# Another order of the first steps, and one pair in four turned by VectorE, in a fused attention and feed-forward kernel

## The chip, the cores and the metric

The kernel runs on one core of one Trainium2 chip. The metric is the device time of one execution in microseconds (us). A core has TensorE (PE in the profile, its weight loads PEld), VectorE (DVE), ScalarE (ACT), GpSimd (POOL) and SyncE (SP), which each work through their own list of instructions in order, and 16 DMA engines that they share.

## The reference

Attention inside chunks of 64 tokens, then a feed-forward block on its result:

```python
scores = scale * np.matmul(q_c, k_c.transpose(0, 1, 2, 4, 3))   # 8 x 8 heads, 576 tokens, chunks of 64, depth 64
scores = scores - np.max(scores, axis=-1, keepdims=True)
attn = np.exp(scores)
attn = attn / (np.sum(attn, axis=-1, keepdims=True) + 1e-09)
out = np.matmul(attn, v_c)
...
xn = (x - mu) / np.sqrt(var + 1e-06) * g_ln                     # x: 4608 tokens x 512
ch = np.maximum(xn @ w_ch1, 0.0) @ w_ch2                        # 512 -> 2048 -> 512
return (x + ch).astype(np.float32)
```

All inputs are float32. The weights reach the kernel as 64-bit words, of which the chip puts the low and the high half together again, and products are made from a high and a low part of each operand, three matmuls for one.

## The kernel before

The 4608 tokens are 18 pairs of 256 tokens, two pairs are a tile, nine tiles in all. The first three tiles (LEAD = 3, pairs 0 to 5) go through an ordinary feed-forward network, in three stretches of program: START, SECOND and THIRD. The other six tiles are done in three units of two tiles, four pairs, each, with a scheme that saves products by sums and differences of blocks.

**Attention** is a generator (`attention`, lines 264 to 560). Each `yield` ends a step, so a caller that holds the generator decides what stands between its steps. The steps of a pair: load q and k; 64 small matmuls for the scores (line 312, into the PSUM tile `s`); the row maxima `top` (line 319) and the load of v; the subtraction and exponential; the turning of the probabilities `p_sb` into `pt_sb`; the sums `den`; 64 small matmuls with the values (line 413); the division into `x`; the statistics (lines 457 and 458); the scaling `xg` (line 469); for the pairs of the units after the first, ScalarE's scaling by `rstd` (line 475), one transpose of 32x32 blocks on VectorE (line 480) and 16 DMAs that put the blocks into `rows`. There are three ways to turn the probabilities. For the first pairs (`by_pe`) TensorE does 8 transposes and ScalarE two copies (lines 362 and 364). In the units TensorE does it in two steps (`pt_by_pe`, lines 372 and 375), or VectorE does it in four steps of four transposes each of 32x256 (line 384). Pairs 0 and 1 (streams a and b) subtract the maxima by a matmul with `minus` (line 339) and take the sums from the matmul with the values, and their `xg` is turned by TensorE (line 522, ScalarE copies at line 525, low parts by line 529 and 532).

**Weights.** `convert_w` (stream w, lines 157 to 241) fetches the blocks in parts (part 0 and 1 are the halves of block 0 and have 512 KB each, part i is block i - 1 and has 1 MB), takes the absolute value on ScalarE (`start_w`, line 171), rounds on VectorE (`round_w`, lines 178, 179 and 182), sets the sign (`sign_w`, line 189) and casts to the high part on ScalarE (line 195); for parts 2 to 10 ScalarE writes the negative of it (line 197) and a GpSimd DMA adds the rounded value to make the low part (`split_w`, line 212); for parts 0 and 1 TensorE does the subtraction (lines 208 and 209). Three raw places and three places for the rounded values are used in turn.

**START** is a string in which each character takes one step of a stream: a and b are the attention of pairs 0 and 1, A and B of pairs 2 and 3, E of pair 4, w the weights, k two matmuls that only keep TensorE busy (`keep_warm`, line 245), u, v and y the products of the feed-forward network (u for pair 0 and v for pair 1 in blocks 0 to 5, y for both from block 6), and 1, 2 and 3 the rectifying and splitting that belongs to u, v and y. A product stream makes the first-layer block 0 and 1 (line 569), the second-layer part of block 0 (line 593), the first-layer block 2, the second-layer part of block 1, and so on. Instructions reach each engine's list in the order of the string. A tile that takes another's place waits until every reader of the other is done.

**Units.** `unit_ffn` makes 4 quarters of 14 products (line 1022), each 6 matmuls of 512 columns, and then 28 pairs of items of the second layer (`double.products`, line 952), 24 matmuls of 256 columns for each pair of items. It counts its work: 6 a product, 3.17 a quarter of a pair of items, 691 in all for one unit. `weave` takes the steps of other streams when the count has passed the position that is written down for them. In unit u the four pairs of unit u + 1 are prepared: pair n begins at BEGINS[n] and its steps stand at BEGINS[n] + PAIR_STEPS[n]; the tuple's length says which way the probabilities are turned (17 steps by TensorE, 19 by VectorE). The load of q and k of the next pair is taken at the begin of each pair. HALVES are the positions at which `combine` makes the operands of the next unit from the turned rows (512 and 612). VectorE's own part of a quarter is six adds (line 1031) and two mixes (line 1039); in the second layer it splits each item (`low`, lines 894 and 898), as a plan says (`double.plan`): item i is rounded (`high`) at i - 4 and split at i - 3.4.

Of the kernel before, what the change touches and what calls it, by code (L numbers as in the profile page):

```python
# [31 lines left out]

START = "kkwkwakwbkwkwkawwwwaawwbwabbkwAkwawbwakkabkkaabaAbabauw1Abbub1Bkbwvuuwuw12wwAvvvw22AwvwvuAvw2wwAvvw1u2AuwwBwvuv12vBuuwyywABA1ww3Ayww3wAywAyuwwwwA3y3BywBBBwBEyyBBwy3w3yywBwwyww3BwwyByy3ywy33yy3E"
LEAD = 3
UNITS = (NTILE - LEAD) // 2

# [10 lines left out]
}  # L49
ROOMS = {1: (3, 9), 2: (6,)}  # L50

BEGINS = (4, 92, 154, 246)
STEPS = (0, 5, 9, 14, 20, 31, 42, 53, 61, 67, 72, 77, 85, 90, 97, 104, 116, 128, 140)
BY_TENSOR = (0, 6, 11, 18, 33, 37, 40, 48, 54, 60, 67, 72, 80, 86, 98, 110, 122)
WIDE = (0, 5, 9, 14, 22, 35, 48, 61, 69, 75, 80, 85, 93, 98, 105, 110, 122, 134, 146)
AT_END = (0, 6, 11, 18, 33, 37, 40, 48, 54, 82, 92, 97, 104, 109, 121, 133, 146)
PAIR_STEPS = (STEPS, BY_TENSOR, WIDE, AT_END)
HALVES = ((512, 8), (612, 10))
MIXING = ((8, 10, 14, 18, 40, 48, 50, 64), (64, 66, 70, 74, 84, 92, 94, 108))
REST = (2, 6, 20)  # L60
# [43 lines left out]
def chunk_attention_ffn(ctx: ExitStack, tc: tile.TileContext, qkv, v01, g, w, out):  # L104
# [1017 lines left out]
    def play(order, streams):  # L1122
        for c in order:
            next(streams[c])
# [33 lines left out]
    with tc.manual_schedule():  # L1158
        nc.scalar.activation(minus, ident, AF.Copy, scale=-1.0)
        play(START, now)  # L1160
        now.update(
# [10 lines left out]
        def following(u, n):  # L1172
            n, u = n % 4, u + n // 4
            if (u, n) not in streams and u < UNITS:
                by_pe = len(PAIR_STEPS[n]) == len(BY_TENSOR)
                streams[u, n] = tiles[LEAD + 2 * u + n % 2].attention(n // 2, pt_by_pe=by_pe)
            return streams.get((u, n), iter(" "))
# [7 lines left out]
        for u in range(UNITS):  # L1185
            if u + 1 < UNITS:
                for n in range(4):
                    begin, steps = BEGINS[n], PAIR_STEPS[n]
                    side += [(begin + at, following(u + 1, n)) for at in steps]
# [41 lines left out]
```

## Time and profile before

| | us |
|---|---|
| median of 3 runs | 827.74 (827.0 to 831.5) |
| the profiled execution | 827.4 |
| its span | 825.6 |
| TensorE busy | 815.5 |
| VectorE busy | 624.4 |
| ScalarE busy | 346.6 |
| GpSimd busy | 202.9 |

The span runs from the first to the last instruction that the hardware profiler recorded. A row of a group gives line, engine, operation, tiles, shapes and count, then the busy time, the mean of one in ns, the idle time of the engine just before and what ended it. A row of the timeline begins with the start in us and the duration in us (several equal instructions are merged, x says how many); what stands in square brackets is the idle time before it and the releaser. The chain of waits lists start, length and what the time was spent on. In the windows each engine has its busy time in the stretch. The granted clock was 0.999 in this run.

### The profile page before, as it was taken

What the parts mean: (1) busy time and instruction counts of PE and PEld (TensorE: products, weight loads), DVE (VectorE), ACT (ScalarE), POOL (GpSimd) and SP (SyncE); (2) the same over time, 40 slices, a digit from 0 to 9 for tenths busy, and PEclk for the clock granted to TensorE, in tenths of its full rate; (3) what the DMA queues carried; (4) which work ended last, traced back from release to release, by engine and by line L of the source; (5) the groups of instructions that cost most, each with busy time, mean ns of one, the idle gap of its engine ahead of it and who ended that gap; (6) DMA issues with size and microseconds to landing.
All of it is one profiled execution on the core that took longest, in us unless ns stands there. A gap on an engine that the chain in (4) does not pass through costs nothing.

```text
span 825.6 us, 16930 instructions
## 1 busy us (share of the span) xinstructions
PE 815.5 (99%) x6746; PEld 711.8 (86%) x6746; DVE 624.4 (76%) x999; ACT 346.6 (42%) x553; POOL 202.9 (25%) x172
## 2 busy tenths in 40 slices
PE   7999999999999999999999999999999999999998
PEld 5888888888888888888899997888999988889998
DVE  6989975787566975879688988797889942249954
ACT  4766432131333432443464542434544532345432
POOL 0111005553857966510000450000002700000000
PEclk9999999999999999999999999999999999999999
DMA  9998315958786349988789669687796586668662
GB/s 359 334 290 231 153 52 192 357 191 282 266 300 224 116 153 384 345 276 281 279 256 345 188 198 345 227 279 255 225 314 210 179 295 192 197 186 291 209 212 102
DMA packets 114366, 201.66 MB, mean 244 GB/s; under 512 B 8432, under 2 KB 75504, under 8 KB 110320
## 3 DMA queue, kind: packets, MB, share of 16 engines
q1 hardware_dynamic: 112992, 195.87, 69.5%
q0 software_dynamic: 1296, 4.72, 2.9%
q8 instruction: 53, 0.87, 0.4%
q14 instruction: 25, 0.20, 0.1%
HBM read 142.88 MB, written 48.76 MB: 232 GB/s over the span
## 4 chain that ended last, share of the span: by engine, by line
PE 92%; DVE 4%; DMA 2%; issue 0%; ACT 0%; SPq 0%; DVEq 0%; ACTq 0%
PE y L952 29%; PE y L1022 26%; PE y L593 15%; PE h L569 15%; PE s L312 2%; PE h L413 1%; DMA wp<-wfs 1%; DMA qk<-qkv 1%; DVE pt_sb L384 1%; PE s L413 1%; PE s L339 0%; PE s L372 0%; PE s L362 0%; DVE hu L1031 0%; PE s L501 0%
## 5 line engine op out<-in xcount | busy, mean ns | idle before, releaser
L1022 PE MATMUL y<-xc,ring 128*128 128x512 f32 x1008 | 235.1, 392 | 0.2 <-DVE hu L1031 0.2
L1022 PEld LDWEIGHTS y<-xc,ring 128*128 128x128 f32 x1008 | 187.5, 188 | 39.8 <-DVE hu L1031 0.6
L952 PE MATMUL y<-ring,hx 128*128 128x256 f32 x1272 | 158.0, 283 | 0.0
L952 PEld LDWEIGHTS y<-ring,hx 128*128 128x128 f32 x1272 | 155.0, 192 | 0.0
L569 PE MATMUL h<-xth,wp 128*128 128x512 f32 (+1 forms) x432 | 129.5, 370 | 0.8 <-DMA wp<-wfs 0.8
L1031 DVE TENSOR_TENSOR hu<-y,snap 128x512 f32<-128x512 f32 x72 | 49.2, 686 | 68.5 <-PE y L1022 34.1
L593 PE MATMUL y<-wp,hh 128*128 128x512 f32 x376 | 96.2, 394 | 0.0
L889 ACT ACTIVATE hx<-hu 128x512 fp32r<-128x512 f32 x106 | 65.6, 630 | 68.0 <-PE y L952 59.9
L569 PEld LDWEIGHTS h<-xth,wp 128*128 128x128 f32 x432 | 78.2, 188 | 15.4 <-DMA wp<-wfs 1.0
L794 POOL TENSOR_TENSOR xc<-rows,xc 128x512 fp32r<-128x512 f32 x28 | 59.9, 2152 | 113.7 <-ACT xc L790 112.1
L593 PEld LDWEIGHTS y<-wp,hh 128*128 128x128 f32 x376 | 69.1, 188 | 13.9
L898 DVE TENSOR_TENSOR hx<-hu,hx 128x512 fp32r<-128x512 f32 x90 | 67.4, 757 | 16.7 <-ACT hx L889 15.2
L569 PE MATMUL h<-xtl,wp 128*128 128x512 f32 (+1 forms) x216 | 78.3, 367 | 0.0
L1028 ACT COPY snap<-y 128x512 f32<-128x512 f32 x72 | 41.6, 585 | 72.0 <-PE y L1022 72.0
L952 PE MATMUL y<-ring,hh 128*128 128x256 f32 x496 | 71.8, 283 | 0.0
L583 DVE SCALAR_TENSOR_TENSOR hl<-h,hh 128x512 fp32r<-128x512 f32 (+1 forms) x53 | 32.9, 627 | 50.1 <-ACT hh L582 49.9
L582 ACT ACTIVATE hh<-h 128x512 fp32r<-128x512 f32 (+1 forms) x53 | 28.6, 546 | 97.5 <-PE h L569 97.4
L952 PEld LDWEIGHTS y<-ring,hh 128*128 128x128 f32 x496 | 65.2, 192 | 0.2
L463 POOL TENSOR_TENSOR rstd<-vare,mhalf 128x2 f32<-128x2 f32 x12 | 10.0, 832 | 175.3 <-DVE vare L462 175.3
L889 ACT ACTIVATE hh<-hu 128x512 fp32r<-128x512 f32 x62 | 38.7, 631 | 31.5 <-PE y L952 28.3
L593 PE MATMUL y<-wp,hl 128*128 128x512 f32 x188 | 51.8, 390 | 0.0
L384 DVE STREAM_TRANSPOSE pt_sb<-p_sb 32x256 f32<-32x256 f32 x112 | 48.8, 436 | 3.6 <-ACT p_sb L348 1.7
(147 smaller groups left out, 1087.9 us busy)
## 6 DMA issues: line engine op xcount, KB each, us to landing
ring<-wa SPq DMA_DIRECT2D x84, 512.0 KB, 5.0
ring<-wb SPq DMA_DIRECT2D x48, 512.0 KB, 4.2
ring<-w2d SPq DMA_DIRECT2D x36, 512.0 KB, 4.0
raw<-w SPq DMA_DIRECT2D x15, 1024.0 KB, 7.8
out<-x SPq DMA_DIRECT2D x22, 512.0 KB, 5.5
qk<-qkv SPq DMA_DIRECT2D x18, 512.0 KB, 6.9
w2d<-wp SPq DMA_DIRECT2D x16, 512.0 KB, 7.5
wa<-parts SPq DMA_DIRECT2D x32, 256.0 KB, 5.5
```

The source lines that it names most:

```text
L384: nc.vector.transpose(out=pt_sb[quad(2 * h2 + j), :, c, quad(i)], in_=p_sb[quad(2 * c + i), :, h2, quad(j)])
L569: nc.tensor.matmul(h, lhsT=(wh, wh, wl)[m][:, ks], rhs=(xth, xtl, xth)[m][:, k, :], start=i == 0, stop=i == len(terms) - 1,)
L582: nc.scalar.activation(hh, h, AF.Relu)
L583: nc.vector.scalar_tensor_tensor(out=hl, in0=h, scalar=0.0, in1=hh.bitcast(F32), op0=ALU.max, op1=ALU.subtract)
L593: nc.tensor.matmul(sums(pairs[j // 2])[j % 2], lhsT=(hh, hh, hl)[m], rhs=(wh, wl, wh)[m], start=f == 0 and m == 0, stop=f == NF - 1 and m ...
L794: engine.tensor_tensor(out=o[:, 1], in0=x, in1=o[:, 0].bitcast(F32), op=ALU.subtract)
L889: nc.scalar.activation(hh, self.split[i][2], AF.Relu if x == "1" else AF.Copy)
L898: nc.vector.tensor_tensor(out=hl, in0=x, in1=hh.bitcast(F32), op=ALU.subtract)
L952: nc.tensor.matmul(bank[j // 2][:, j % 2 * PAIR : (j % 2 + 1) * PAIR], lhsT=(hh, hh, hl)[m][:, j * P : (j + 1) * P], rhs=loaded[t // 2][:, ...
L1022: nc.tensor.matmul(bank, lhsT=w[:, (0, 0, 1)[m], ks], rhs=x[:, (0, 1, 0)[m], k, :], start=start and k == m == 0, stop=k == 1 and m == 2, s ...
L1028: nc.scalar.copy(out, bank)
L1031: nc.vector.tensor_tensor(out=out, in0=bank, in1=s, op=ALU.add)
```

## The change

The first 125 or so characters of START are in another order (three k fewer; from `ww3Ayww3` on the two strings are equal). The load of pair 0 is issued ahead of the first weights, one of the k steps behind it; the turning of pair 0's probabilities comes ahead of the fourth part's absolute value; all turning steps of pair 0's `xg` come before pair 1's division; and pair 1's first transposes stand ahead of the first product of u. In the units the second pair uses STEPS instead of BY_TENSOR, so VectorE turns its probabilities in four steps, and the third and fourth pair begin at 190 and 282 instead of 154 and 246, with steps as before.

```diff
-START = "kkwkwakwbkwkwkawwwwaawwbwabbkwAkwawbwakkabkkaabaAbabauw1Abbub1Bkbwvuuwuw12wwAvvvw22AwvwvuAvw2wwAvvw1u2AuwwBwvuv12vBuuwyywABA1ww3Ayww3wAywAyuwwwwA3y3BywBBBwBEyyBBwy3w3yywBwwyww3BwwyByy3ywy33yy3E"
+START = "awkwkwkbkkwwkawwkwwkawabwawAbbawwbwwakkbaaaaaAbabbbuw1ABub1bwkbuuvwuw1v2wwAvvw22AwvvAvvwwAu2vwwuwv21AuwwwBuuy12BvvA1wuAywBww3Ayww3wAywAyuwwwwA3y3BywBBBwBEyyBBwy3w3yywBwwyww3BwwyByy3ywy33yy3E"
...
-BEGINS = (4, 92, 154, 246)
+BEGINS = (4, 92, 190, 282)
 STEPS = (0, 5, 9, 14, 20, 31, 42, 53, 61, 67, 72, 77, 85, 90, 97, 104, 116, 128, 140)
 BY_TENSOR = (0, 6, 11, 18, 33, 37, 40, 48, 54, 60, 67, 72, 80, 86, 98, 110, 122)
 WIDE = (0, 5, 9, 14, 22, 35, 48, 61, 69, 75, 80, 85, 93, 98, 105, 110, 122, 134, 146)
 AT_END = (0, 6, 11, 18, 33, 37, 40, 48, 54, 82, 92, 97, 104, 109, 121, 133, 146)
-PAIR_STEPS = (STEPS, BY_TENSOR, WIDE, AT_END)
+PAIR_STEPS = (STEPS, STEPS, WIDE, AT_END)
```

## The prediction

> **What bounds the kernel now.** I read the page first, then TensorE's list of waits from 60 us to the end, then the chain of waits, and last the instructions in order of time, for the first 60 us and for the second unit.
>
> ```profile
> span 825.6 us, 16930 instructions
> PE 815.5 (99%) x6746; PEld 711.8 (86%) x6746; DVE 624.4 (76%) x999; ACT 346.6 (42%) x553; POOL 202.9 (25%) x172
> PE y L1022 <- DVE hu L1031: 0.2, 1, 0.2
> ```
>
> The third line is the whole list of TensorE's waits after 60 us. From there on TensorE is the bound, and its work comes off the time one for one, as long as no new wait opens. Ahead of 60 us the chain of waits looks different:
>
> ```profile
> 2.11 6.86 DMA qk<-qkv
> 44.38 9.65 DMA wp<-wfs
> 66.82 1.43 PE h L569 x12
> 92.42 1.09 PE s L413 x64
> ```
>
> It runs through pair 0's load and VectorE's list, and that part ends in the transfer that adds block 4's low half in (split_w, line 212). The product of block 4 waits for that until 54.08; after that TensorE works almost without a hole (the last two rows are pieces of its work, for their length). So the first part of the change is worth what it does to this landing, and to the TensorE work that still stands behind it.
>
> **The first steps.** The rows in time:
>
> ```profile
> 0.74 0.85 SPq L155 DMA_DIRECT2D raw<-w  x2
> 1.64 1.00 SPq L280 DMA_DIRECT2D qk<-qkv  x2
> 2.39 6.09 PE L245 MATMUL y<-minus 128*128 128x512 f32 x14 [2.39 <-ACT minus L1159]
> 4.88 0.67 ACT L171 ACTIVATE wf<-raw 128x512 f32<-128x512 f32 x1 [2.54 <-DMA raw<-w]
> 5.58 0.43 DVE L178 TENSOR_SCALAR wf<-wf 128x512 f32<-128x512 f32 x1 [5.58 <-ACT wf L171]
> 6.25 0.69 ACT L171 ACTIVATE wfs<-raw 128x512 f32<-128x512 f32 x1 [0.71 <-DMA raw<-w]
> SPq L332 <- DMA qk<-qkv: 1.1, 1, 1.1
> 7.68 0.33 SPq L332 DMA_DIRECT2D g_sb<-g  x1
> 9.11 1.16 PE L312 MATMUL s<-qk 64*64 64x64 f32 x64 [0.62 <-DMA qk<-qkv]
> 10.33 1.23 DVE L319 TENSOR_REDUCE top<-s 128x16 f32<-128x1024 f32 x1 [0.89 <-PE s L312]
> 15.94 1.23 DVE L319 TENSOR_REDUCE top<-s 128x16 f32<-128x1024 f32 x1 [0.65 <-PE s L312]
> 16.46 1.15 ACT L171 ACTIVATE wf<-raw 128x1024 f32<-128x1024 f32 x1 [1.30 <-DMA raw<-w]
> 17.98 1.08 ACT L364 COPY pt_sb<-y 128x512 f32<-128x512 f32 x2
> ```
>
> The first four loads are 512 KB each and land in the order of their issue: by 4.88, 6.25, 7.68 (what the queue's g_sb waited for) and 9.11 at the latest, one per 1.4 us. The new order issues q and k of pair 0 first. Then q and k are there at 6.3, and the first weights at 7.7 instead of 4.9. The loads behind these four are not moved, since the same bytes stand ahead of them.
>
> What uses them does not change places: in both orders VectorE does round 0, sign 0, round 1, and only then pair 0's top. Before, this work took from 5.58 to 9.44 (10.33 less 0.89 idle), 3.8 us without a hole. Now it begins 0.7 after its load, at 8.4, and the top starts at 12.2 instead of 10.33: 1.8 late, though the scores would be done by 9 (12 warming matmuls of 0.435, 6.09 / 14, end at 7.6; scores take 1.2). From the first top to the second are 5.6 us through TensorE and ScalarE, as before, so all of VectorE's list is 1.8 late from there. ScalarE now copies pair 0's turned probabilities (1.08) ahead of the fourth abs (16.46 in the rows); that abs ends at about 20.4, where VectorE wants it at 20.0: 2.2 late in all.
>
> ```profile
> 30.55 1.38 DVE L469 SCALAR_TENSOR_TENSOR xg<-x,mv,g_sb 128x512 f32<-128x512 f32 x2
> 34.91 1.02 PEld L569 LDWEIGHTS h<-xth,wp 128*128 128x128 f32 x8 [0.15 <-DVE hl L583]
> 35.77 1.17 ACT L171 ACTIVATE wfs<-raw 128x1024 f32<-128x1024 f32 x1
> 40.63 1.22 DVE L189 SCALAR_TENSOR_TENSOR wfs<-raw,wfs 128x1024 uint32<-128x1024 uint32 x1
> 44.38 0.89 POOL L212 DMA_DIRECT2D wp<-wfs  x1 [3.59 <-DVE wf L179]
> 54.08 0.30 PEld L569 LDWEIGHTS h<-xth,wp 128*128 128x128 f32 x2 [0.98 <-DMA wp<-wfs]
> 58.30 0.19 PEld L569 LDWEIGHTS h<-xth,wp 128*128 128x128 f32 x1 [0.44 <-DVE hl L583]
> DMA to landing us min/median/max: 6.4/7.6/9.7
> ```
>
> Then ScalarE adds 0.6. In the old order pair 1's last copy stands ahead of the abs of 35.77, in the new one behind it, so that copy (half of a 1.08) falls between the abs and the casts of the next block, and the rectified blocks that VectorE splits ahead of sign 5 stand behind those casts. Sign 5 (40.63) comes 2.8 late, and so does the issue of block 4's transfer: 47.2. It landed after 9.65 before; the transfers that share the engines with it (the next raw weights) shift with it, so the same again gives 56.8, and the median of 7.6 gives 54.8: **0.7 to 2.8 late**.
>
> TensorE is there first. Its first products stand behind pair 1's first transposes in the new order: pair 1's xg has its first half at 30.55 + 0.7 + 2.2 = 33.4; four transposes (0.4) and two first-layer blocks (1.4 each) end at 36.6, and the rest of pair 1's transposes and splits, with a keep_warm step, at about 38. The old order had done the same list at 34.91 or 35.0: 3.0 late. But by the landing it has less to do: the order takes the waiting product (the eighth v, token 86 instead of 96, counted from 0) ahead of pair 2's 64 products with the values (1.09) and one first-layer block (1.43). Those 2.5 us were done under the wait before, and now come after it. In exchange the 0.44 of 58.30 is lost in the longer wait. The first steps: between 0.7 + 2.5 - 0.4 = 2.8 and 2.8 + 2.5 - 0.4 = 4.9; I take the middle, **+3.8**. The lower bound, if no landing holds TensorE at all: its own late start of 3.0 less the waits that are gone, 0.98 and 0.44, +1.6. The three keep_warm steps that go cost nothing either way in this sum: they stood in gaps.
>
> **The units.** The second pair (n = 1) occurs in units 0 and 1, each time for the next unit.
>
> ```profile
> 351.65 7.03 PE y L1022 x30
> 358.69 0.87 PE s L372 x8
> 528.49 0.87 PE s L372 x8
> 352.78 0.69 DVE L1031 TENSOR_TENSOR hu<-y,snap 128x512 f32<-128x512 f32 x1 [1.82 <-POOL mixed L1006]
> 356.79 0.68 DVE L1031 TENSOR_TENSOR hu<-y,snap 128x512 f32<-128x512 f32 x1
> 356.90 1.06 ACT L348 ACTIVATE p_sb<-p_sb 128x1024 f32<-128x1024 f32 x1 [1.61 <-DVE p_sb L345]
> 357.38 1.28 DVE L1039 SCALAR_TENSOR_TENSOR hu<-hu 128x512 f32<-128x512 f32 x2
> 374.51 1.78 DVE L384 STREAM_TRANSPOSE pt_sb<-p_sb 32x256 f32<-32x256 f32 x4
> 328.61 15.19 PE y L1022 x66
> 522.75 0.69 DVE L1031 TENSOR_TENSOR hu<-y,snap 128x512 f32<-128x512 f32 x1 [1.76 <-ACT snap L1028]
> ```
>
> Removed: 2 x 0.87 of TensorE, on the path, -1.74; and ScalarE's two copies, off it. Added on VectorE: 16 transposes in four steps of 1.8 (1.78 and the start of the next), 7.2 per pair, off the path as long as pair 1's 64 products with the values find their operand. Here I add up the steps of unit 0. VectorE is late already when pair 1 begins: the add due with its scores ran at 352.78, and top, pair 0's last transpose, the subtraction and an add bring it to 357.4, and ScalarE's exponential (356.90 + 1.06) to 358.0. Then in the order of the counts: four groups of transposes (7.2), two mixes (0.6 each), two adds (0.6 each): 358.0 + 9.6 = 367.6. TensorE needs it at step 159, which falls after count 162: 66 matmuls after the scores, 351.65 + 15.19 = 366.8. So it waits 0.8. In unit 1 everything stands 170.0 later on VectorE (522.75) and 169.8 on TensorE: 1.0. The next add, which frees a bank for the last matmuls of this quarter, ends 0.6 after the transposes, behind those 64 products, and holds nothing. **-1.74 + 1.8 = about 0**; with all of it hidden -1.7.
>
> The Trainium skill, "VectorE: DVE Perf Modes", section "Rules for kernel authors", says to turn 128x128 blocks on TensorE where PSUM will do as the destination, since VectorE turns blocks of 32x32 only. That speaks against the change; the trace agrees on the price of one pair (7.2 us against 0.87), and the sum by that rule would be a loss wherever VectorE's 7.2 are not covered.
>
> Third and fourth pair move by 36 counts, and their loads, spills and scatter DMAs on SP with them; both still end before the combining at 512 and 612, so no queue order is turned round that anyone waits for. But the fourth pair now multiplies, normalises and turns inside the second-layer products:
>
> ```profile
> 416.00:421.00 5.00, 5.00 (x44) 5.00 (x44) 5.00 (x8) 3.87 (x7) 0.00 (x0) 1.00 0.94 254
> 414.67 80.63 PE y L952 x672
> ```
>
> VectorE (the third busy number) is full there already. The splits of the plan (low) are issued 3.4 items ahead of their use, at 80.63 / 56 = 1.44 us an item 4.9 us. Five short steps of the fourth pair (two statistics, two scalings, one transpose) arrive at counts 364 to 387 instead of 328 to 350, when the lead is built up. I put this at 0, and if the lead is eaten, at a few us.
>
> **Sum:** the profiled execution took 827.4 (span 825.6 and 1.8 around it; the median of the runs is 827.74, so it is a typical one): 827.4 + 3.8 + 0 = **831.2**.
>
> **Rivals.** (1) *VectorE becomes the bound of the units* (slower). If its lateness passes the 4.9 us of lead, each split comes late and TensorE waits for VectorE, in both units. For it: the full row above. Against: over both stages VectorE is busy 76% of the span, and the work only moves by 36 counts. At 2 us a unit: 835.2. It decides once pair 1's turning ends 2 us later than I added up, or the lead is gone. (2) *The load of pair 0 was what held the start* (faster): the chain of waits names it first. If the top came right after scores at 7.6 + 1.2, 1.4 earlier than 10.33, and the turning were hidden: 827.4 - 1.4 - 1.7 = 824.3. Against it stands VectorE's order, with round 1 ahead of the top. (3) *The change of order is nearly absorbed*: block 4 lands when the transfers let it, not when it is issued; only the lower bound is left: 827.4 + 1.6 + 0 = 829.0. For it: the spread of 6.4 to 9.7 between equal transfers. (4) *TensorE's clock gate falls back*, as fewer warming matmuls stand in the gaps. The row of 14 took 435 ns each, and the scores at 9.11 already ran at the pace of later ones (1.16 for 64, against the 1.09 of 92.42); the largest hole I find in the new order is 2 us. If it fell back, the 3 us of products before block 4 would double: 834. The Trainium skill, "TensorE: Matmul & The Clock Gate", section "Part 1: The HAM clock gate", gives 426.7 ns cold and 215.7 warm for 512 columns and an idle window of 3.4 us; the row of 14 agrees with cold.
>
> **Chances.** Forecast 0.48 (its own range 829.5 to 833), rival 1 0.18, rival 2 0.12, rival 3 0.17, rival 4 0.05. About 0.5% (4.1 us) is what a measurement of this kernel can tell from no change: slower than 831.9 are rivals 1 and 4 and a third of the forecast, 0.39; faster than 823.6 is a good half of rival 2, 0.07; the rest, 0.54, lies between. The range of 824.3 to 836 leaves out that half of rival 2 and the far end of rival 1.
>
> **What would show it.** In the new profile the first top at 12.2, the second at 17.8; block 4's transfer issued near 47 and a TensorE wait of 1 to 4 us for it; no L372 in the second pair and 32 more rows of L384; waits of about 1 us ahead of L413 in the units, once in each. I am wrong if the first top stands near 9, if the transfer's landing is no later than 54.1, or if the second-layer products wait for hl or hx.

## The result, and the profile after

The changed kernel takes 833.81 us (median of 7 runs, 833.15 to 836.47) against 827.92 for the kernel before on the same chip (7 runs, 827.0 to 831.5): a ratio of 1.0075 [1.0063, 1.0088], **slower by 0.75%**. The forecast of 831.2 lies 2.6 below it, and the forecast's own range of 829.5 to 833 ends 0.8 below it; a time slower than 831.9 had been given a chance of 0.39. The profiled execution of the changed kernel took 836.2 (span 834.4) and is one of the two slowest of the seven: at a mean granted clock of 0.998 these took 836.2 and 836.5, the other five, at 0.999 to 1.000, 833.2 to 834.2. What the two have more is seen below.

The page, and TensorE's list of waits from 45 us to the end (line, the two tiles and the releaser; us in total, times, longest), in the kernel after:

```profile
span 834.4 us, 16930 instructions
PE 814.8 (98%) x6724; PEld 709.7 (85%) x6724; DVE 638.3 (76%) x1031; ACT 344.8 (41%) x549; POOL 204.5 (25%) x172
PE y L1022 <- ACT snap L1028: 2.5, 2, 1.3
PE h L569 <- DMA wp<-wfs: 1.9, 1, 1.9
PE h L413 <- DVE pt_sb L384: 0.9, 2, 0.4
PE h L569 <- DMA wp<-wf: 0.2, 1, 0.2
```

TensorE is busy for 0.7 us less than before, and yet the span is 8.8 longer. The two lines with DMA belong to the first steps, the other two to the units. The third was forecast, with twice its size. The first, the largest in total, wasn't: ScalarE's copy `snap`, once in each of two units.

The first steps after, in order of time (start, duration, then the work, and in brackets the idle time before it and what ended it):

```profile
7.56 0.67 ACT L171 ACTIVATE wf<-raw 128x512 f32<-128x512 f32 x1 [5.22 <-DMA raw<-w]
12.04 1.22 DVE L319 TENSOR_REDUCE top<-s 128x16 f32<-128x1024 f32 x1
17.64 1.23 DVE L319 TENSOR_REDUCE top<-s 128x16 f32<-128x1024 f32 x1 [1.19 <-PE s L312]
33.32 0.66 PE L522 MATMUL y<-ident,xg 128*128 128x128 f32 x4 [1.27 <-DVE xg L469]
47.27 0.89 POOL L212 DMA_DIRECT2D wp<-wfs  x1 [3.88 <-DVE wf L179]
55.63 0.50 PE L569 MATMUL h<-xth,wp 128*128 128x256 f32 x2 [1.94 <-DMA wp<-wfs]
57.09 1.99 PE L413 MATMUL s<-v_t,pt_sb 64*64 64x64 f32 x64
```

The first weights come at 7.56 instead of 4.88, the two tops at 12.04 and 17.64, block 4's transfer is issued at 47.27 and TensorE resumes at 55.63, after an idle time of 1.94. The last row is new: 64 products with the values take 1.99, where before they took 1.16 (51.71). The windows over that place (busy time of each engine, then the granted clock PEclk, the share of the DMA engines and GB/s) say why:

```profile
54.00:56.00 2.00, 0.37 (x3) 0.37 (x4) 1.99 (x3) 0.79 (x3) 0.87 (x1) 1.00 0.99 389
56.00:58.00 2.00, 2.00 (x42) 1.79 (x44) 1.16 (x2) 1.97 (x3) 0.00 (x0) 0.72 1.06 223
58.00:60.00 2.00, 2.00 (x47) 1.88 (x41) 1.78 (x3) 1.07 (x2) 0.85 (x1) 0.50 0.99 295
60.00:62.00 2.00, 2.00 (x14) 1.86 (x13) 0.28 (x1) 0.38 (x1) 0.01 (x1) 0.93 1.13 293
```

From about 57 to 60 the granted clock is 0.50. That is the clock gate of rival 4, but behind the wait for block 4. Windows of half a microsecond at both ends give the stretch more exactly:

```profile
56.50:57.00 0.50, 0.50 (x5) 0.38 (x4) 0.20 (x1) 0.50 (x2) 0.00 (x0) 0.88 1.25 238
60.00:60.50 0.50, 0.50 (x5) 0.50 (x4) 0.00 (x0) 0.00 (x0) 0.01 (x1) 0.71 0.83 319
```

The mean of 0.88 puts the fall to 0.50 at 56.88, the mean of 0.71 the return at 60.29: 3.4 us.

Where the units begin, in the chain of waits (start, length), the first three rows before and the last three after:

```profile
326.16 1.36 PE y L1022 x6
495.30 1.39 PE y L1022 x6
665.11 76.19 PE y L1022 x336
332.06 1.36 PE y L1022 x6
502.58 1.39 PE y L1022 x6
673.94 76.19 PE y L1022 x336
```

So of the 8.8 the first steps make 5.9, unit 0 takes 170.52 instead of 169.14 (1.4 more) and unit 1 171.36 instead of 169.81 (1.6 more). Behind that nothing changes.

### The profile page after: what moved, and what is told of

It reads as the page before. It is cut to its first block, busy times and chain, and to the rows that moved or that the text cites. A ratio compares the mean times of both kernels' runs of the same rounds, so it can differ in the third digit from the quotient of the medians.

```text
span 834.4 us, 16930 instructions
## 1 busy us (share of the span) xinstructions
PE 814.8 (98%) x6724; PEld 709.7 (85%) x6724; DVE 638.3 (76%) x1031; ACT 344.8 (41%) x549; POOL 204.5 (25%) x172
## 4 chain that ended last, share of the span: by engine, by line
PE 89%; DVE 5%; DMA 3%; ACT 1%; issue 1%; SPq 0%; DVEq 0%; ACTq 0%
PE y L952 29%; PE y L1022 24%; PE h L569 15%; PE y L593 15%; DVE pt_sb L384 2%; PE s L312 2%; PE h L413 1%; DMA wp<-wf 1%; DMA v_t<-qkv 1%; DMA raw<-w 1%; DVE hu L1031 1%; PE s L413 1%; PE s L362 0%; PE s L501 0%; DVE den L391 0%
## 5 line engine op out<-in xcount | busy, mean ns | idle before, releaser
L384 DVE STREAM_TRANSPOSE pt_sb<-p_sb 32x256 f32<-32x256 f32 x144 | 62.7, 436 | 5.0 <-ACT p_sb L348 2.7
L889 ACT ACTIVATE hh<-hu 128x512 fp32r<-128x512 f32 x62 | 38.7, 631 | 31.4 <-PE y L952 28.8
```

The costliest lines, as they stand in the source:

```text
L384: nc.vector.transpose(out=pt_sb[quad(2 * h2 + j), :, c, quad(i)], in_=p_sb[quad(2 * c + i), :, h2, quad(j)])
L889: nc.scalar.activation(hh, self.split[i][2], AF.Relu if x == "1" else AF.Copy)
```

## The experiments

Each is compared with the kernel before on its own chip: 828.05 for the first eight, 827.73 for the last three. Where only a stretch of START differs, the diff shows that stretch.

**The first steps alone** (e1) and **the units alone** (e2).

```diff
-START = "kkwkwakwbkwkwkaw...        e1: START of after, units of before
+START = "awkwkwkbkkwwkaww...
-BEGINS = (4, 92, 154, 246)          e2: START of before, units of after
+BEGINS = (4, 92, 190, 282)
-PAIR_STEPS = (STEPS, BY_TENSOR, WIDE, AT_END)
+PAIR_STEPS = (STEPS, STEPS, WIDE, AT_END)
```

> The new order of the first steps with the units as before. Theory A (the late first weights and the waiting product taken early cost the time, and TensorE's half rate behind that wait): 3.5 to 6 us over before, the first unit beginning 3.5 to 6 us later, TensorE waiting 1 to 3 us for block 4's transfer. Rival B (the units cost nearly all): within 1.5 us of before.

> The old order of the first steps with VectorE turning the second pair and the third and fourth pair 36 counts later. Theory A: 2 to 3 us over before, 1.2 to 1.6 for each of units 0 and 1, in which TensorE waits once for ScalarE's copy behind the exponential and once for the last turned quarter. As predicted on record: 0. Rival B: 4 to 6 us over before.

Measured: 831.98, a ratio of 1.0047 [1.0032, 1.0061], and 830.42, 1.0026 [1.0015, 1.0038]. The first steps cost 3.9, the units 2.4, and the sum of 6.3 is about the 5.9 of the whole change. So the forecast had the sum of the first steps right (+3.8), and the units wrong by their whole loss (0). In e1 TensorE waits twice for a low half, and its clock stays full:

```profile
54.73 0.50 PE L569 MATMUL h<-xth,wp 128*128 128x256 f32 x2 [0.42 <-DMA wp<-wfs]
69.45 0.73 PE L569 MATMUL h<-xth,wp 128*128 128x512 f32 x2 [0.35 <-DMA wp<-wfs]
```

The wait for block 4 is well under the 1 to 3 us that e1's theory A gave for it. A third wait of 0.54, at 386.90 in unit 0, is for a load of the units' own weights (`ring`), so a part of e1's 3.9 may lie behind the first steps. In e2 the list of waits has the same two kinds as the kernel after (2.5 for `snap`, 0.9 for the turning).

**Only the load of pair 0 moved** (e3): START of before with its first `a` put at the front.

```diff
-START = "kkwkwakwbk...
+START = "akkwkwkwbk...
```

> The old order with one character moved: the load of pair 0 ahead of everything. Units as before. Theory A1 (the late first weights are a cost by themselves): the first top near 12.0 instead of 10.3, block 4's transfer 1.5 to 2.5 us late, 1.5 to 3 us over before. Rival A2 (the loads' order is absorbed, the cost is in the places of the products): within 0.5 us of before.

Measured: 830.53, 1.0042 [1.0024, 1.006]. The move alone costs 2.5. The first top is at 12.02, as forecast, the second at 19.13, later than in the whole new order, because TensorE's subtraction of the maxima runs at half the pace there:

```profile
13.30 3.50 PE L339 MATMUL s<-top,minus 128*128 128x512 f32 x4 [1.24 <-DVE top L319]
```

The same four matmuls took 1.98 in the kernel after. The granted clock is 0.50 from 13 to 16 here. Block 4's transfer is issued at 47.58, 3.2 late, where 1.5 to 2.5 had been expected: the 1.5 that the half clock costs is part of the 2.5.

**Only the third and fourth pair moved** (e4).

```diff
-BEGINS = (4, 92, 154, 246)
+BEGINS = (4, 92, 190, 282)
```

> The old order, the second pair turned by TensorE as before, but the third and fourth pair 36 counts later. Theory: the shift costs nothing, within 0.5 us of before, and no wait in the units. Rival (the fourth pair in the second-layer products makes the splits late): 1 to 3 us over before, with waits of TensorE for hx or hl.

Measured: 827.5, 0.9992 [0.9983, 1.0001], and no new wait. The shift costs nothing, as forecast, full as VectorE is there.

**The waiting product put back** (e5): START of after, with the eighth `v` behind pair 2's products with the values and a first-layer block, as the old order had it; units of before.

```diff
-...22AwvvAvvwwAu2vwwu...
+...22AwvvAvwwAu2vvwwu...
```

> The new order of the first steps, but the waiting product of block 4 (the eighth v) behind pair 2's products with the values and the first-layer block that stood behind it; units as before. If the work that was put behind the wait is the cost (a term of the prediction, 2.5 us): 1.5 to 2.5 us under the new order alone, so 829.5 to 830.5. If TensorE's late first product is the cost: the wait is gone but the time within 0.7 us of the new order alone (831.98).

Measured: 831.2, 1.0036 [1.0022, 1.005], 0.8 less than e1, though 2.5 us of work had been put under the wait again. The two intervals overlap, and in the profiled executions unit 0 begins at 329.93 here and at 329.90 in e1, so no gain is shown. The wait for block 4 is gone, and the next low half holds TensorE in its place: it resumes at 69.47 (0.58 idle) where in e1 it resumed at 69.45. The end of the first steps hangs on two landings one behind the other; covering the first leads to the second.

**The weights' loads ahead again** (e6): START of after, its first eight characters with pair 0's load behind the first two parts.

```diff
-START = "awkwkwkbkkww...
+START = "wkwkawkbkkww...
```

> The new order of the first steps with its first eight characters changed so that the first weights are loaded ahead of pair 0; units as before. Theory A1 (the late first weights are half of the cost or more): the first top back near 10.3, block 4's transfer issued near 45.5, 829 to 830.3. Rival A2 (the places of the products are the cost): 831.3 to 832.5.

Measured: 830.68, 1.0027 [1.0016, 1.0038]. That takes away 1.3 of e1's 3.9 by the medians (the intervals overlap), and unit 0 begins 1.7 earlier than in e1 (328.17). The first top is back at 10.37 and block 4's transfer is issued 1.7 earlier than in e1:

```profile
10.37 1.23 DVE L319 TENSOR_REDUCE top<-s 128x16 f32<-128x1024 f32 x1 [0.91 <-PE s L312]
46.19 0.89 POOL L212 DMA_DIRECT2D wp<-wfs  x1 [3.87 <-DVE wf L179]
53.02 0.50 PE L569 MATMUL h<-xth,wp 128*128 128x256 f32 x2 [0.40 <-DMA wp<-wfs]
67.71 0.73 PE L569 MATMUL h<-xth,wp 128*128 128x512 f32 x2 [0.32 <-DMA wp<-wfs]
```

Block 4 is even there before the 54.08 of the kernel before, and the kernel is still 2.6 slower: what is left of the loss lies in the order behind the loads.

**The second pair's steps spaced** (e7): START of before, and VectorE's turning in the second pair with a tuple of its own, SPACED. Against STEPS its exponential stands 8 counts later, the turning 7 to 10, the products with the values 14.

```diff
+SPACED = (0, 6, 11, 22, 27, 39, 51, 63, 69, 81, 87, 93, 99, 104, 106, 112, 124, 136, 148)
-BEGINS = (4, 92, 154, 246)
+BEGINS = (4, 92, 190, 282)
-PAIR_STEPS = (STEPS, BY_TENSOR, WIDE, AT_END)
+PAIR_STEPS = (STEPS, SPACED, WIDE, AT_END)
```

> The old order of the first steps, VectorE turning the second pair, third and fourth pair 36 counts later, but the second pair's exponential 8 counts later, its turning groups 12 counts apart behind the adds of the quarter, and its products with the values 14 counts later. Theory: both waits of each unit (ScalarE's copy behind the exponential, the last turned quarter) are gone and the 2 x 0.87 us of TensorE's transposes show: 826 to 827, 1 to 2 us under before. Rival (VectorE is simply full, the wait moves elsewhere): 829.5 to 831.

Measured: **826.16**, 0.9972 [0.9961, 0.9982], faster than both kernels. No wait of TensorE is left in the units but one of 0.2, and unit 0 takes 168.45 (326.08 to 494.53) instead of 169.14.

**Only the exponential later** (e8): START of before, units of after, with the second pair's exponential 4 counts later and nothing else.

```diff
+EXP_LATER = (0, 5, 9, 18, 20, 31, ...             e8, against the units of after
-PAIR_STEPS = (STEPS, STEPS, WIDE, AT_END)
+PAIR_STEPS = (STEPS, EXP_LATER, WIDE, AT_END)
```

> The old order of the first steps with the units' change, and only the second pair's exponential 4 counts later, so that it stands behind ScalarE's copy of the fourth product. Theory: TensorE's wait for that copy (1.2 in each unit) is gone; part of it comes back ahead of the products with the values, so 0.8 to 1.8 us under the units' change alone (830.4). Rival (the copy's wait is not ScalarE's order): no change from 830.4.

Measured: 828.5, 1.0002 [0.9991, 1.0013]. Four counts for one step take away 1.9 of the 2.4 that the units cost. TensorE's list of waits in the units, with lines one higher than in the other kernels:

```profile
PE h L414 <- DVE pt_sb L385: 1.0, 2, 0.5
PE y L1023 <- DVE hu L1032: 0.4, 2, 0.2
```

The wait for `snap` is gone, and the wait for VectorE's turning is left, once in each unit, where the prediction had put it.

**Three more orders of the first steps**: e9 is e6 with pair 1's first transposes put back behind the first product; e10 is e9 with the eighth `v` and the first `y` put back behind other work; e11 is e10 with the units of e7.

```diff
-...abbbuw1AB...       e9, against e6
+...abbubw1AB...
-...vvAvvwwAu2vwwu...Buuy12BvvA1wu...       e10, against e9
+...vvAvwwAu2vvwwu...Buu12BvvyA1wu...
```

> The new order of the first steps with the weights' loads ahead again (830.7 in the last run, 2.6 over before), and pair 1's first transposes moved back behind the first step of u; old units. TensorE waited 1.28 for pair 1's xg ahead of its first product. Theory A (TensorE's own late start is what is left): the first product starts at 31.0 to 31.4 instead of 32.67 and the time falls by 1.2, to about 829.4. Theory B (the landings of the low halves hold TensorE again as soon as it is earlier): the first product starts as early, but the wait for block 4's low half grows from 0.4 to about 1.6 and the time stays at 830.7, within 0.4.

> As the run before, and the two products that wait for low halves put back behind other work: the eighth v behind A and u, and the first y behind three steps of v, as they stood before the change; old units. Theory B: both waits for wp (0.4 and 0.3 in the last run, grown to some 1.6 by the earlier start) are covered, and the time is 828.5 to 829.3. Theory A: no more than the run before, 829.4. If a third thing holds the first steps (the second top is 0.6 late, by pair 0's turning), it stays above 829.5 though no wait for wp is left.

> The first steps of the run before with the spaced units (826.16 with the old first steps, 1.9 under before). The parts add up so far, so 1.9 under the run before: 826.6 to 827.4. It would beat the spaced units alone only if the run before is faster than before.

Measured: 832.66 (1.0055 [1.0036, 1.0074]), 833.72 (1.0065 [1.0044, 1.0087]) and 831.69 (1.0033 [1.0014, 1.0052]). All three came out slower than either theory gave, by 2 to 5 us (that e11 is 2.0 under e10 was as expected), and they scatter: e11 from 825.8 to 834.0. The profiled executions of e9 and e10 are the slowest of their kernels (837.1 and 836.6). In all three profiles the clock falls to half already at the start, behind a hole of 2.0 to 2.2 us ahead of the scores, which in e6 was 1.39 and left the clock full; in e10:

```profile
9.18 1.92 PE L312 MATMUL s<-qk 64*64 64x64 f32 x64 [2.15 <-DMA qk<-qkv]
```

The scores took 1.16 in e6, whose second top came at 16.57; here and in e9 it comes at 18.2. So the first product of e9 begins at 32.40, where 31.0 to 31.4 had been expected, and its wait for block 4 is 1.53, near the 1.6 of theory B. The profile of e10 then shows the wait for block 4 covered, and this:

```profile
54.00 11.41 DMA wp<-wf
65.45 0.79 PE L569 MATMUL h<-xth,wp 128*128 128x256 f32 x2 [5.46 <-DMA wp<-wf]
```

```profile
60.00:65.00 5.00, 0.00 (x0) 0.00 (x0) 1.56 (x2) 0.00 (x0) 0.00 (x0) 0.89 0.98 240
65.00:70.00 5.00, 4.55 (x21) 4.55 (x22) 2.61 (x3) 3.14 (x3) 0.86 (x1) 0.50 0.75 259
```

The first row of the upper fence is a piece of the chain: the transfer after block 4's, 512 KB as all of them, took 11.41 to land; the lower fence has the windows. In e6 the same transfer landed 5.0 after its issue. TensorE stood for 5.46, ScalarE and most of the time VectorE stood too, and then the next five microseconds ran at a granted clock of 0.50. e9 and e11 wait for the same transfer, 3.94 and 2.55. The mean clocks of e11's executions go with their times only roughly: those at 0.999 and 0.997 took 825.8 and 827.7, those at 0.995 and 0.996 took 831.6 to 834.0, but the two at 0.998 took 830.3 and 831.6. So neither theory's time came true, and these three runs do not decide between A and B: in the profiled executions the time goes to one late transfer and to the half clock behind two holes, and what the orders would be worth without them is not shown.

## Why the prediction was right and wrong

**The first steps were right in most of their rows; their sum was right in part by luck.** Each step had a forecast: first top 12.2 (12.04), second top 17.8 (17.64), issue near 47.2 (47.27), landing between 54.8 and 56.8 (55.63 after, 54.73 in e1), pair 1's transposes from 33.4 (33.32), a wait of 1 to 4 (1.94 after, but 0.42 in e1), and +3.8 in all (3.9 in e1). The split into landing and deferred work shows in the time from block 4's product to unit 0 (in us; "issue" is that of block 4's transfer, "between" the time from TensorE's resuming to unit 0):

| kernel | issue | TensorE resumes | unit 0 begins | between |
|---|---|---|---|---|
| before | 44.38 | 54.08 | 326.16 | 272.1 |
| e3, old order with the load moved | 47.58 | 57.10 | 329.17 | 272.1 |
| e6, new order, weights first | 46.19 | 53.02 | 328.17 | 275.2 |
| e1, new order | 47.88 | 54.73 | 329.90 | 275.2 |
| after | 47.27 | 55.63 | 332.06 | 276.4 |

The new order has 3.1 more behind the landing. The forecast had 2.1 (2.5 of deferred work less 0.4); the waits of 0.3 to 0.4 for the next low half and the 0.2 to 0.3 that a wait costs beyond its row add to that, and some 0.4 stays without an account. The landing itself is 0.65 late in e1 and 1.55 in the profiled execution of after; the sum's middle stood for 1.75. So in e1 the landing is 1.1 smaller than the sum had it and the work behind it 1.0 larger, and the two errors cancel.

Counted by TensorE alone, the loss of e1 is there before block 4's transfer is issued: from 40 us to unit 0 TensorE is busy for 289.1 us in e1 and 285.4 before, 3.7 more, and idle for 0.8 in both. The prediction had this late start at 3.0, and expected the old waits of 0.98 and 0.44 to go; waits of the same sum came in their place.

And after has another 1.2 over e1: at half clock from 57 to 60, TensorE did 1.5 us of work in 3. With the landing, 0.9 later than in e1, that makes 2.1 of the 2 to 3 by which the profiled execution is over the five faster ones of after. The second execution with this clock and time has no profile, so that it lost the time in the same way is likely but not shown.

**The sum for the units left out a queue.** The prediction counted TensorE's 1.74 less, and two waits of 0.8 and 1.0 for VectorE's turning. e8 shows these two where they were put, somewhat smaller: 0.5 each in the list of waits, with about 0.3 more each in the starts, and a time equal to before. What it did not count is ScalarE's own list. STEPS has the exponential at 14, BY_TENSOR has it at 18: at count 106 instead of 110, and that is enough to put it ahead of the copy for the fourth product of the quarter. One row of ScalarE in unit 0 before, and then the rows of three engines after:

```profile
354.70 0.59 ACT L1028 COPY snap<-y 128x512 f32<-128x512 f32 x1 [2.00 <-PE y L1022]
```

```profile
357.48 5.74 PE L1022 MATMUL y<-xc,ring 128*128 128x512 f32 x24
361.59 1.19 DVE L345 TENSOR_TENSOR p_sb<-s,top 128x1024 f32<-128x1024 f32 x1
362.81 1.06 ACT L348 ACTIVATE p_sb<-p_sb 128x1024 f32<-128x1024 f32 x1 [4.21 <-DVE p_sb L345]
363.77 1.54 ACT L1028 COPY snap<-y 128x512 f32<-128x512 f32 x3
364.37 0.69 DVE L1031 TENSOR_TENSOR hu<-y,snap 128x512 f32<-128x512 f32 x1 [1.60 <-ACT snap L1028]
364.39 9.86 PE L1022 MATMUL y<-xc,ring 128*128 128x512 f32 x42 [1.17 <-ACT snap L1028]
374.19 0.34 PE L413 MATMUL h<-v_t,pt_sb 64*64 64x64 f32 x6
374.95 1.14 PE L413 MATMUL h<-v_t,pt_sb 64*64 64x64 f32 x58 [0.43 <-DVE pt_sb L384]
```

Before, ScalarE makes the copy at 354.70, 28.5 after the unit's begin, and the exponential (356.90, quoted in the prediction) after it. After, the exponential runs as late in the unit as before, 30.7 after its begin, since VectorE's subtraction is no earlier; but ScalarE stands idle in front of it for 4.21 us, and the copy comes behind it, at 363.77, 31.7 after the begin. TensorE waits 1.17 for that copy's bank, VectorE 1.60 for the copy itself, and the turning ends 1.1 later in the unit than in e8. One subtraction that isn't there yet is passed on to all three engines through one queue. The step of the prediction that failed is this one: it went through VectorE's list in order and named what waits behind what, and of ScalarE it counted only the two copies that go, without asking what stands behind the exponential in ScalarE's list. In unit 0 the 24 matmuls of 357.48, at 0.23 each, would have let the next begin at 363.0, and they begin at 364.39, 1.4 later; the 64 products last from 374.19 to the end of the 1.14 at 374.95, about 0.7 more than their 1.16 before. 1.4 and 0.7, less 0.9 for the transposes that go, make 1.2 of the 1.4 by which the unit grew.

**The rivals.** Rival 1's time (835.2) is nearer than the forecast's, and it had TensorE waiting for VectorE in both units, but its place was the lead of the splits in the second layer, and no wait for `hl` or `hx` occurs there; the shift is free (e4). What it priced, pair 1's turning ending later than added up, did happen, but by way of ScalarE and by 1.4 (counted from the begin of the unit), less than the 2 that it asked for. Rival 2 is refuted by e3 and e6: moving the load of pair 0 forward costs 1.3 (e6) to 2.5 (e3, with 1.5 of half clock in it). Rival 3 was right on the landing for the greater part: in e1 the transfer is issued 3.5 later than before and lands 0.65 later, and in e6 1.8 later and 1.1 earlier. Its price of +1.6 was wrong, since the late start was 3.7 and the waits didn't go. Rival 4's time (834) is the nearest of all, by luck: it named the right mechanism at the wrong place, with 3 us lost ahead of block 4, where the trace has 1.5 lost behind it. The prediction looked for holes ahead of block 4 and did not ask what the hole that it forecast itself, the wait of up to 4 us, would do to the clock behind it. The Trainium skill, "TensorE: Matmul & The Clock Gate", section "Part 1: The HAM clock gate", gives a free-running window of 3.4 us. That the half clock lasts 3.4 us in after agrees with it, while the hole ahead of it was only 1.94 long, with busy time on both sides.

**What stays open.** Why one and the same transfer lands after 5.0 in e1 and e6, 9.9 in after and 11.4 in e10. In all of them a raw load of 1 MB, the values of one pair (twice 256 KB) and the next such transfer are under way beside it, and the DMA engines are full; which of them goes first was not separated. Nor was the 2.6 by which e6 is still over before taken apart further than the table does.

## What to carry to other kernels

A step that is issued a few counts earlier on an engine with plenty of idle time is not free: look at what stands behind it in that engine's list, and when its operand is really there. When a hole on TensorE is forecast, price the time behind it too (here up to 1.5 us behind a wait of 1.94), and when a wait is covered, look for the next transfer that will end last. An order that lives on the landing of a transfer should be measured over many executions, since the landing may scatter by more than the order is worth.

## What the runs showed of the hardware that was not expected

- A hole of 1.94 us on TensorE was followed by a granted clock of 0.50 (64 products 1.99 instead of 1.16), in e3 holes of 2.03 and 1.24 close together (four matmuls 3.50 instead of 1.98), in e10 one of 2.15 and one of 5.46. The half clock lasts 3.4 us in after, in e3 and in e11 behind its wait of 2.55, and twice that behind the long waits of e9 and e10 (in e10 from 63.9 to 70.8).
- The length of a hole alone doesn't decide: in after itself a hole of 2.07 ahead of 10.75 left the clock at 1.00, as did the holes of 1.17 in the units and of 1.53 in e9. In the 3.4 us ahead of each half-clock stretch TensorE was busy for 1.5 us or less (after 1.47, e3 1.33; e9, e10 and e11 at the start 1.39, 1.25 and 1.33, and behind the low halves 1.06, 0 and 1.39). Stretches of 3.41 us counted back from the fall at 56.88 in after cut the hole of 2.07 so that TensorE is busy for 1.76 in the stretch from 9.10 to 12.51. So the busy share of fixed stretches fits these cases; that is inferred from them, and no run tests it.
- A wait costs TensorE 0.2 to 0.3 more than its row says (1.17 in the row and 1.4 in the starts, 0.43 and 0.7).
- Equal adding transfers of 512 KB took from 4.4 (the last one of before and after) to 11.7 us (in e9) to land. The range of block 5's alone, from 5.0 in e1 and e6 to 11.7, was found with the DMA engines full.
